# Retention and ELU feed-forward on one core: q decayed on GpSimd, outputs copied out of PSUM by ScalarE

## The chip, the core and the metric

The kernel runs on one core of a Trainium2 chip. The metric is the device time of one execution in microseconds (us). The engines are TensorE (PE in the profile, with its weight loads as PEld), VectorE (DVE), ScalarE (ACT), GpSimd (POOL) and SyncE (SP), which issues the DMAs.

## What is computed

The reference is a recurrent retention block followed by a feed-forward block with an ELU. Batch is 4, there are 8 heads of 64 channels, the sequence is 768 long; the 3072 tokens of 512 channels then pass through 512 x 2048 and 2048 x 512 weights.

```python
gamma = 1.0 - 2.0 ** (-5.0 - np.arange(H))
for t in range(S):
    state = gamma * state + k[:, :, t] (x) v[:, :, t]      # outer product, per head
    y[:, :, t] = scale * q[:, :, t] @ state
x = y.transpose(0, 2, 1, 3).reshape(B * S, H * D)
h = x @ w_in
g = np.where(h > 0.0, h, np.exp(np.minimum(h, 0.0)) - 1.0)
out = g @ w_out
```

## The kernel before

The tokens are worked off in six blocks of 512 (`tb` 0 to 5), each of four chunks of 128 tokens. A chunk's q, k and v lie in one tile `chunk` (128 x 2048 float32; four buffers), loaded by one DMA; q and k are in it with channels on the partitions, v and a second k with tokens on the partitions.

The decay is not applied step by step. With positions counted within a sequence, v is multiplied by gamma to the power of minus its position (`scale_v`, line 286, table `vf`), and the result of retention by gamma to the power of its position. The second factor lies in the table `etab` (128 x 4 x 768), which `powers_of` (line 254) fills with ScalarE exponentials at the start: first its first 256 columns, later the other 512. Retention of a block is `scores` (products of k and q, masked by VectorE), `states` (products of k and v added to a running state) and `outputs` (for each pair of chunks, products into two PSUM tiles `y`, first within the chunk, then against the states). At the end of `outputs`, line 398, VectorE multiplies each `y` with its piece of `etab` and writes the block's feed-forward input, `xb` (or `xt` for block 1).

Work is ordered by hand (a manual schedule): each engine runs its instructions in the order in which the program's generators are interleaved. Retention of block tb + 1 is placed in steps between the feed-forward products of block tb.

Block 0's first product is plain: `plain_first` makes 16 tiles of 128 x 512, each of four 128 x 512 matmuls (lines 511 and 535). The PSUM banks go round: tiles 0 to 3 use pa, pa, pb, pd (pa is two buffers), tile 4 a bank called hp, tiles 5 to 8 again pa, pa, pb, pd, and so on. Each tile is followed by `elu`: two ScalarE instructions (line 491 a Relu out of the bank into `r`, line 492 an Exp), and, one tile later in VectorE's order, line 495, which reads `r` and the bank and so releases it. Between the tiles the weights of the feed-forward block are decoded: `prepare` (lines 164 to 168, ScalarE) and `decode` (lines 190 to 194, VectorE) work on pieces `wraw`. GpSimd scales the four v chunks of block 1 there.

Later blocks use two levels of Strassen's scheme with products of 128 x 128 (lines 885 and 973) and of 128 x 256 (line 931); ScalarE copies `ms` and `m` and VectorE additions (lines 899, 939, 985) empty their banks, VectorE subtractions (lines 847, 944) make their inputs. In the loop over blocks `bring(n)` loads chunk n of the next block and has GpSimd scale its v.

Of the kernel before, what the change touches and what calls it, by code (L numbers as in the profile page):

```python
# [9 lines left out]
FP32 = mybir.dt.float32  # L10
# [3 lines left out]
AF = mybir.ActivationFunctionType  # L14
ALU = mybir.AluOpType
# [3 lines left out]
def kernel(  # L19
# [32 lines left out]
    nc = tc.nc  # L52
    PSUM = bass.MemoryType.PSUM
    P = nc.NUM_PARTITIONS

    B, H, S, D, DM, DFF = dims
    NTOK = B * S
    C = P
    TB = 512
    TH = TB // 2  # L60
    HP = H // 2
    NCH = S // C
    NCHUNK = NTOK // C
    NTB = NTOK // TB
    CPB = TB // C
# [3 lines left out]
    scale = 1.0 / math.sqrt(D)  # L69
# [143 lines left out]
    for a in range(2):  # L213
        for u in range(2):
            for c in range(2):
                nc.vector.memset(lny[c * D : (c + 1) * D, a, u : u + 1], math.log(gammas[head(a, u, c)]))
    pos_s = const.tile([P, NCH, H], I32, name="pos_s")
    nc.gpsimd.iota(pos_s, pattern=[[C, NCH], [0, H]], base=0, channel_multiplier=1)
    begin = so_.rearrange("p n s c -> p (n s c)")
# [26 lines left out]

    post = begin[:, S : 2 * S]
    nc.vector.tensor_copy(post, pos_t)
    etab = const.tile([P, 2, 2, S], FP32, name="etab")

    def powers_of(tokens):
        for a in range(2):
            for u in range(2):
                nc.scalar.activation(etab[:, a, u, tokens], post[:, tokens], AF.Exp, scale=lny[:, a, u : u + 1])

    powers_of(slice(0, 2 * C))

# [22 lines left out]
    def scale_v(m, by_vector=False):  # L280
        if m >= NCHUNK:
            return
        i = chunks[m][1]
        v = raw[m][1][:, 0]
        eng = nc.vector if by_vector or m < 2 else nc.gpsimd
        eng.tensor_tensor(  # L286
            out=v, in0=v, in1=vf[:, i].unsqueeze(2).to_broadcast([C, H, D]), op=ALU.mult
        )

    rows = lambda n: slice(n * D, (n + 1) * D)  # L290

# [86 lines left out]
    def outputs(tb, pp):  # L378

        y = [ps_r.tile([P, 2 * 2, 2, D], FP32, name="y", tag="r") for _ in range(2)]  # L380
        for x in range(2):
            for j in range(4):
                pt = raw[tb * CPB + 2 * pp + j // 2][0][:, 1].rearrange("p h c -> p (h c)")
                within(tb, pp, x, j, y, lambda p: pt[:, (x * HP + p) * D :][:, 0:D])
        for other in range(2):
            if not other:
                yield
            else:

                for sub in range(2):  # L390
                    seen = epool.tile([P, 8], FP32, name="seen", tag="seen")
                    nc.vector.tensor_copy(seen.rearrange("p (j x) -> p j x", x=2), y[sub][:, :, :, 0])
                yield
            for x in range(2):
                across(tb, pp, x, other, y)
        i = chunks[tb * CPB + 2 * pp][1]
        for sub in range(2):
            nc.vector.tensor_tensor(
                out=place_of(x_of(tb)[:, :, 2 * pp * C : 2 * (pp + 1) * C])[:, :, :, sub, :], in0=y[sub],
                in1=place_of(powers[:, :, i * C : (i + 2) * C])[:, :, :, sub, :], op=ALU.mult,  # L400
            )

    def within(tb, pp, x, j, y, pt):
        kv = raw[tb * CPB + 2 * pp + x][1]
# [759 lines left out]
    take()  # L1164
    state_sum(kvs, 0, 0, 1, 1)
    prepare(2)
    powers_of(slice(2 * C, S))
    next(inner)
    piece = decode()
    take()  # L1170
# [36 lines left out]
    for n, _ in enumerate(inner):  # L1207
        if n in (0, 2, 4):
            load(CPB + n // 2)
        if n == 4:  # L1210
            load(CPB + 3)
        if n in (1, 2, 4, 5, 7, 9):
            next_piece(n in (1, 2, 5, 7))
        if n in (3, 5, 7, 9):
            scale_v(CPB + (n - 3) // 2)
        if n == 4:
            run(inputs_of_first(0, [hslot() for _ in range(3)]))
        elif n == 10:
            scores(1, 0)
            scores(1, 1)  # L1220
        elif n == 11:
            states(1, 0)
            states(1, 1)
            next_piece()
            parts = sums_of_pieces(0)
            next(parts)
        elif n == 12:
            outputs_step(1, 0)
            run(parts)
            next_piece()  # L1230
        elif n == 13:
            outputs_step(1, 1)
            smalls = small_of_pieces(0)
            some(smalls, 3)
        elif n == 14:
            outputs_step(1, 2)
            some(smalls, 2)
            decode_all()
        elif n == 15:
            run(smalls)  # L1240
# [63 lines left out]
    for n in range(NQ):  # L1304
        if n < 3:
            load(2 * CPB + n)
        if n == 2:
            load(2 * CPB + 3)
        cur = first(n)
        for at in range(3):  # L1310
            next(cur)

        if n in (1, 2):
            some(smalls[n + 1], 1)
        elif n == 3:
            scale_v(2 * CPB, True)
        for _ in tail:
            pass
        for at, s in enumerate(cur):
            next(sides[n], None)  # L1320
            next(sides[n], None)
            if at == 1 and n in (0, 2):
                some(smalls[2 if n == 0 else 3], 2)
            elif at == 1 and n == 3:
                for m in range(1, CPB):
                    scale_v(2 * CPB + m, True)
            if s == "gap":
                break
        for _ in sides[n]:
            pass  # L1330
        tail = cur
        if n in (1, 2):
            run(smalls[n + 1])
        send_small()
# [28 lines left out]
    for tb in range(2, NTB):  # L1363
        more = tb + 1 < NTB
        qa, qd, u2, end = {}, {}, {}, None

        def rest(n, j):
            if j == 1:
                qa[n] = ps_r.tile([P, 2, TH], FP32, name="qa", tag="r") if n == 0 else bank("a")
            if j == 7:  # L1370
                qd[n] = ps_r.tile([P, 2, TH], FP32, name="qd", tag="r") if n == 3 else bank("bd"[n % 2])
            first_rest(n, j, qa[n] if j in (1, 6, 5) else qd[n])

        def bring(n):
            if more:
                load((tb + 1) * CPB + n)
                scale_v((tb + 1) * CPB + n)

        def pop(count=1):
            for _ in range(count):  # L1380
                if later:
                    later.pop(0)()

        bring(0)
        rest(0, 1)
        for _ in tail:
            pass
        tail, parts = iter(()), combine_x_parts()
        for at, j in enumerate(TWICE):
            cur = first_twice(tb, j)  # L1390

            next(cur)
            next(tail, None)
            next(parts, None)
            next(cur)
            for _ in tail:
                pass
            next(parts, None)
            if at == 1:

                first_end(0, "C11", qa[0])()
                bring(1)
            next(cur)
            tail = cur
        next(tail)
        bring(2)

        sec = second_twice(tb, combine_x_twice if more else lambda: None)
        for n in range(NQ):

            rest(n, 6)
            u2[n] = kept(qa[n])
            if n == 0:
                for _ in tail:
                    pass
            if end:
                end()
            pop()
            rest(n, 7)
            m7 = kept(qd[n])  # L1420
            pop(2)
            if n == 2 and more:
                retention_step(tb + 1, 1)
            if n == 3:
                next(sec)
            rest(n, 5)
            end = first_end(n, "C12", qa[n])
            other = first_end(n, "C22", qa[n], m7)
            if n < 3:
                end()  # L1430
                other()
                rest(n + 1, 1)
                first_end(n + 1, "C11", qa[n + 1])()
                rest(n, 4)
                end = first_end(n, "C21", qd[n], u2[n])
                pop()
                if n == 0:
                    bring(3)
                elif n == 1 and more:
                    retention_step(tb + 1, 0)  # L1440
        for _ in range(2):
            next(sec)
        end()
        other()
        rest(3, 4)
        end = first_end(3, "C21", qd[3], u2[3])
        next(sec)
        end()
        flush()
        step = 0  # L1450
        for s in sec:

            if s == "first":
                step += 1
            elif s != "middle" and step in (1, 4, 5):
                retention_step(tb + 1, {1: 2, 4: 3, 5: 4}[step])
            if s == ORDER2[-1]:
                break
        tail = sec
# [51 lines left out]
```

## Time and profile before

| what | value |
|---|---|
| three runs | 632.18, 632.34, 633.39 us; median 632.34 us |
| span of the profiled execution, first to last instruction | 631.6 us |
| the execution's own time beside the span | not given apart; the median lies 0.74 us above the span |
| TensorE busy | 623.8 us, 99% |
| VectorE busy | 482.1 us, 76% |
| ScalarE busy | 255.3 us, 40% |
| GpSimd busy | 22.1 us, 4% |
| granted TensorE clock | 0.999 |
| line 398, `y` times `etab` on VectorE | 22 instructions of 128 x 512, 0.68 us each |
| line 286, v scaling on GpSimd | 16 instructions of 128 x 512, mean 1212 ns |

Times in a row of a timeline are: start within the span, duration, engine, line, operation, output from input, shape, count, and in brackets the idle time before it with what ended it. A group of instructions that follow one another is one row. Busy shares of TensorE come from modelled ends of pipelined matmuls.

### The profile page before, as it was taken

What the parts mean: (1) busy time and instruction counts of PE and PEld (TensorE: products, weight loads), DVE (VectorE), ACT (ScalarE), POOL (GpSimd) and SP (SyncE); (2) the same over time, 40 slices, a digit from 0 to 9 for tenths busy, and PEclk for the clock granted to TensorE, in tenths of its full rate; (3) what the DMA queues carried; (4) which work ended last, traced back from release to release, by engine and by line L of the source; (5) the groups of instructions that cost most, each with busy time, mean ns of one, the idle gap of its engine ahead of it and who ended that gap; (6) DMA issues with size and microseconds to landing.
All of it is one profiled execution on the core that took longest, in us unless ns stands there. A gap on an engine that the chain in (4) does not pass through costs nothing.

```text
span 631.6 us, 16140 instructions
## 1 busy us (share of the span) xinstructions
PE 623.8 (99%) x6678; PEld 560.5 (89%) x6678; DVE 482.1 (76%) x882; ACT 255.3 (40%) x476; POOL 22.1 (4%) x30
## 2 busy tenths in 40 slices
PE   8999999999999999999999999999999999999997
PEld 6864578888899999888999989999989999988997
DVE  6688789989799665799585589777489877558975
ACT  6798646025541114553112646112465211366311
POOL 1021000000000000200000100000110000000000
PEclk9999999999999999999999999999999999999999
DMA  8698669699288788306888702889810698700794
GB/s 329 260 416 295 186 202 268 196 272 319 113 266 257 234 258 315 141 2 199 257 258 296 278 2 71 268 280 289 317 64 16 220 310 252 207 17 4 239 309 151
DMA packets 75897, 136.32 MB, mean 216 GB/s; under 512 B 6320, under 2 KB 31792, under 8 KB 70832
## 3 DMA queue, kind: packets, MB, share of 16 engines
q1 hardware_dynamic: 75824, 135.29, 64.9%
q8 instruction: 53, 0.87, 0.5%
q14 instruction: 20, 0.16, 0.1%
HBM read 114.03 MB, written 21.23 MB: 214 GB/s over the span
## 4 chain that ended last, share of the span: by engine, by line
PE 98%; DVE 0%; issue 0%; ACT 0%
PE pa L973 20%; PE pa L931 10%; PE pd L973 10%; PE pb L973 5%; PE pa L885 5%; PE pb L931 4%; PE pa L758 4%; PE pa L535 3%; PE qa L931 3%; PE x L625 3%; PE pd L885 2%; PE qd L931 2%; PE pd L931 2%; PE pd L758 2%; PE pa L625 2%; PE kv L352 2%
## 5 line engine op out<-in xcount | busy, mean ns | idle before, releaser
L981 ACT COPY ms<-pa 128x128 f32<-128x128 f32 x104 | 27.6, 265 | 148.2 <-PE pa L973 148.2
L973 PE MATMUL pa<-ts,wq 128*128 128x128 f32 x560 | 74.2, 275 | 0.0
L973 PE MATMUL pd<-ts,wq 128*128 128x128 f32 x552 | 73.5, 276 | 0.0
L973 PEld LDWEIGHTS pa<-ts,wq 128*128 128x128 f32 x560 | 68.5, 192 | 0.4
L973 PEld LDWEIGHTS pd<-ts,wq 128*128 128x128 f32 x552 | 67.1, 192 | 0.6 <-DVE res L985 0.2
L973 PE MATMUL pa<-gC,wq 128*128 128x128 f32 x480 | 64.6, 278 | 0.0
L492 ACT ACTIVATE r<-r 128x512 f32<-128x512 f32 x96 | 60.5, 631 | 3.1
L973 PEld LDWEIGHTS pa<-gC,wq 128*128 128x128 f32 x480 | 59.0, 192 | 1.3
L491 ACT ACTIVATE r<-gC 128x512 f32<-128x512 f32 x64 | 39.9, 624 | 31.9 <-DVE gC L939 31.9
L985 DVE TENSOR_TENSOR res<-pd,ms 128x128 f32<-128x128 f32 x68 | 19.5, 287 | 39.6 <-PE pd L973 38.4
L495 DVE SCALAR_TENSOR_TENSOR gC<-r,gC 128x512 f32<-128x512 f32 x64 | 42.6, 697 | 0.7 <-ACT r L492 0.7
L847 DVE TENSOR_TENSOR ts<-gC,ts 128x512 f32<-128x512 f32 x60 | 41.3, 688 | 1.0
L847 DVE TENSOR_TENSOR ts<-gC 128x512 f32<-128x512 f32 x60 | 41.0, 683 | 0.0
L286 POOL TENSOR_TENSOR chunk<-chunk,vf 128x512 f32<-128x512 f32 x16 | 19.4, 1212 | 429.6 <-DMA chunk<-in_qkv_dram 429.6
L973 PE MATMUL pb<-gC,wq 128*128 128x128 f32 x240 | 31.7, 275 | 0.0
L1006 ACT COPY res<-pa 128x128 f32<-128x128 f32 x34 | 9.0, 265 | 55.1 <-PE pa L973 55.1
L973 PEld LDWEIGHTS pb<-gC,wq 128*128 128x128 f32 x240 | 29.2, 192 | 0.0
L704 ACT COPY m<-pa 128x512 f32<-128x512 f32 x24 | 14.0, 582 | 33.0 <-PE pa L758 18.7
L939 DVE TENSOR_TENSOR gC<-qa,gC 128x512 f32<-128x512 f32 x8 | 5.5, 692 | 25.0 <-PE qa L931 18.3
L931 PE MATMUL pa<-xt,w_s 128*128 128x256 f32 x96 | 23.0, 382 | 0.0
L931 PE MATMUL pa<-xt,w_b 128*128 128x256 f32 x96 | 23.0, 382 | 0.0
L931 PE MATMUL pa<-xb,w_a 128*128 128x256 f32 x96 | 22.7, 379 | 0.0
(262 smaller groups left out, 1247.4 us busy)
## 6 DMA issues: line engine op xcount, KB each, us to landing
wq<-scratch_dram SPq DMA_DIRECT2D x277, 256.0 KB, 4.4
chunk<-in_qkv_dram SPq DMA_DIRECT2D x22, 1024.0 KB, 8.7
wraw<-in_w_dram SPq DMA_DIRECT2D x15, 1024.0 KB, 6.0
out_dram<-res SPq DMA_DIRECT2D x14, 256.0 KB, 4.1
scratch_dram<-gT SPq DMA_DIRECT2D x12, 256.0 KB, 4.3
scratch_dram<-m SPq DMA_DIRECT2D x12, 192.0 KB, 6.1
scratch_dram<-so SPq DMA_DIRECT2D x4, 512.0 KB, 4.7
scratch_dram<-wi SPq DMA_DIRECT2D x2, 1024.0 KB, 6.5
```

The costliest lines, as they stand in the source:

```text
L286: eng.tensor_tensor(out=v, in0=v, in1=vf[:, i].unsqueeze(2).to_broadcast([C, H, D]), op=ALU.mult)
L491: nc.scalar.activation(e, h, AF.Relu, scale=-1.0)
L492: nc.scalar.activation(e, e, AF.Exp, scale=-1.0)
L495: nc.vector.scalar_tensor_tensor(g, e, -1.0, h, ALU.add, ALU.max)
L625: nc.tensor.matmul(X[j][:, d, :], lhsT=w[j][:, d * P : d * P + P], rhs=x[j], start=(n == 0 and d == 0), stop=at_end, skip_group_check=True,)
L758: nc.tensor.matmul(ps[:, fi, :], lhsT=w[:, fi, j2, :], rhs=x[:, j2, :], start=(begin and fi == 0 and j2 == 0), stop=(j2 == 1), skip_group_ ...
L847: sub = lambda o, x, y: nc.vector.tensor_tensor(out=o, in0=x, in1=y, op=ALU.subtract)
L885: nc.tensor.matmul(ps[:, f, :], lhsT=lhs[f], rhs=xs[j][k], start=(begin and f == 0), stop=True, skip_group_check=True,)
L931: nc.tensor.matmul(ps[:, fi, :], lhsT=w[:, fi, j2, :], rhs=x[:, j2, :], start=(j in (1, 7) and fi == 0 and j2 == 0), stop=(j2 == 1), skip_ ...
L973: nc.tensor.matmul(ps, lhsT=w[:, f, :], rhs=ts[j][k][:, f, :], start=(begin and f == 0), stop=(f == 3), skip_group_check=True,)
L981: nc.scalar.copy(m, ps)
L985: nc.vector.tensor_tensor(out=o, in0=x, in1=y, op=ALU.add)
```

## The change

From block 1 on, the factor of q moves from the output to q itself. A new table `qtab` (128 x 4 x 768) holds gamma to the power of the position in q's layout; `scale_q` multiplies a chunk's q with it on GpSimd. In the loop over blocks it is called right behind `scale_v`. Block 1's four calls and the table's four exponentials stand between the tiles of block 0's plain product; block 2's four calls stand in the last quarter of block 1's first product. `outputs` then writes `y` with a plain ScalarE copy for every block but block 0. `etab` needs 512 columns only and is laid into a buffer that is used otherwise later.

```diff
+    lnq = const.tile([P, HP], FP32, name="lnq")
+    for a in range(2):
+        for p in range(HP):
+            nc.vector.memset(lnq[a * D : (a + 1) * D, p : p + 1], math.log(gammas[2 * p + a]))
...
-    etab = const.tile([P, 2, 2, S], FP32, name="etab")
+    etab = gq["T3"].rearrange("p (a u x) c -> p a u (x c)", a=2, u=2)
+    qtab = const.tile([P, HP, S], FP32, name="qtab")
...
+    def powers_for_q(p):
+        nc.scalar.activation(qtab[:, p, :], post, AF.Exp, scale=lnq[:, p : p + 1])
...
+    def scale_q(m):
+        if m >= NCHUNK:
+            return
+        i = chunks[m][1]
+        q = raw[m][0][:, 0]
+        nc.gpsimd.tensor_tensor(out=q, in0=q, in1=qtab[:, :, i * C : (i + 1) * C], op=ALU.mult)
...
+        tokens = slice(2 * pp * C, 2 * (pp + 1) * C)
         for sub in range(2):
-            nc.vector.tensor_tensor(
-                out=place_of(x_of(tb)[:, :, 2 * pp * C : 2 * (pp + 1) * C])[:, :, :, sub, :], in0=y[sub],
-                in1=place_of(powers[:, :, i * C : (i + 2) * C])[:, :, :, sub, :], op=ALU.mult,
-            )
+            to = place_of(x_of(tb)[:, :, tokens])[:, :, :, sub, :]
+            if tb:
+                nc.scalar.copy(to, y[sub])
+            else:
+                nc.vector.tensor_tensor(
+                    out=to, in0=y[sub], in1=place_of(powers[:, :, tokens])[:, :, :, sub, :], op=ALU.mult
+                )
...
-    powers_of(slice(2 * C, S))
+    powers_of(slice(2 * C, TB))
...
         if n in (3, 5, 7, 9):                       # between the tiles of the plain product
             scale_v(CPB + (n - 3) // 2)
+            scale_q(CPB + (n - 3) // 2)
+        if n in (0, 1):
+            powers_for_q(2 * n)
+            powers_for_q(2 * n + 1)
...
         elif n == 3:                                # block 1's first product
             scale_v(2 * CPB, True)
+            for m in range(CPB):
+                scale_q(2 * CPB + m)
...
                 scale_v((tb + 1) * CPB + n)         # bring(n) in the loop over blocks
+                scale_q((tb + 1) * CPB + n)
```

More of the change, by code (lines that the diff above doesn't have):

```diff
@@ L395, in outputs @@
                 across(tb, pp, x, other, y)
-        i = chunks[tb * CPB + 2 * pp][1]
+        tokens = slice(2 * pp * C, 2 * (pp + 1) * C)
         for sub in range(2):
-            nc.vector.tensor_tensor(
-                out=place_of(x_of(tb)[:, :, 2 * pp * C : 2 * (pp + 1) * C])[:, :, :, sub, :], in0=y[sub],
-                in1=place_of(powers[:, :, i * C : (i + 2) * C])[:, :, :, sub, :], op=ALU.mult,
-            )
+            to = place_of(x_of(tb)[:, :, tokens])[:, :, :, sub, :]
[5 more added lines that the diff above has]
+                )
     def within(tb, pp, x, j, y, pt):
```

## The prediction

> **What bounds the kernel now.** I read the page first (busy shares, chain), then the waits of TensorE, then the timelines of ScalarE and VectorE where those engines have no idle time, and last TensorE around the same moments.
>
> ```profile
> PE 623.8 (99%) x6678; PEld 560.5 (89%) x6678; DVE 482.1 (76%) x882; ACT 255.3 (40%) x476; POOL 22.1 (4%) x30
> ...
> PE 98%; DVE 0%; issue 0%; ACT 0%
> ```
>
> The chain that ended last is TensorE for 98% of the span. The change leaves TensorE's instructions and their order as they are, so it can act only through time in which TensorE waits. TensorE's list of waits:
>
> ```profile
> PE pa L1124 <- DVE blank L208: 1.5, 1, 1.5
> PE y L423 <- issue: 1.3, 1, 1.3
> PE pd L423 <- DVE seen L440: 0.5, 2, 0.3
> ```
>
> After start-up (first 30 us) only the 1.3 us row remains, a pause with no visible releaser at 298 us. So no VectorE relief, however large, has a wait to remove there: 22 output evictions of about 0.68 us hide under TensorE today. What has to be found is a place where the added or moved work makes TensorE wait. The page's slices (ScalarE 40% busy overall) do not show one; a window table does:
>
> ```profile
> 37.00:51.00 14.00, 14.00 (x35) 6.24 (x34) 11.39 (x15) 13.74 (x18) 5.92 (x4) 1.00 1.00 423
> ```
>
> Columns after the window: TensorE, weight loads, VectorE, ScalarE, GpSimd. Between 37 and 51 us ScalarE is busy 13.74 of 14 us. This is block 0's plain first product, and here the change puts four new ScalarE instructions, the q tables. ScalarE and VectorE there:
>
> ```profile
> 32.33 0.60 ACT L491 ACTIVATE r<-pa 128x512 f32<-128x512 f32 x1 [0.47 <-PE pa L511]
> ...
> 39.48 0.57 ACT L491 ACTIVATE r<-pd 128x512 f32<-128x512 f32 x1
> 40.09 0.63 ACT L492 ACTIVATE r<-r 128x512 f32<-128x512 f32 x1
> ```
> ```profile
> 40.75 0.69 DVE L495 SCALAR_TENSOR_TENSOR gC<-r,pd 128x512 f32<-128x512 f32 x1 [2.40 <-ACT r L492]
> 41.36 0.69 DVE L190 TENSOR_SCALAR wraw<-wraw 128x1024 f32<-128x1024 f32 x1
> 42.08 0.71 DVE L191 TENSOR_SCALAR wraw<-wraw 128x1024 uint32<-128x1024 uint32 x1
> 42.82 1.94 DVE L194 CUSTOM_DVE_ANT_0 w_b<-wraw,w_b 128x2048 uint16<-128x2048 uint16 x1
> ...
> 48.06 0.94 DVE L191 TENSOR_SCALAR wraw<-wraw 128x1024 uint32<-128x1024 uint32 x1
> 49.03 1.23 DVE L194 CUSTOM_DVE_ANT_0 w_a<-wraw,w_a 128x2048 uint16<-128x2048 uint16 x1
> 50.17 1.28 DVE L495 SCALAR_TENSOR_TENSOR gC<-r,pa 128x512 f32<-128x512 f32 x2
> ```
> ```profile
> 47.61 3.60 PE L535 MATMUL pd<-xb,w_a 128*128 128x512 f32 x8
> 51.04 3.60 PE L535 MATMUL pa<-xb,w_a 128*128 128x512 f32 x8
> ```
>
> VectorE waits 2.40 us for ScalarE's exponential of tile 3 (bank pd), and from 40.75 on has no idle time until both ELU ends at 50.17. The first of these two releases the bank pa that TensorE fills again from 51.04. It ends at 50.17 + 0.68 = 50.85: TensorE is 0.19 us from waiting. This is the thinnest slack I found after start-up.
>
> **The change, part by part.** *q tables.* Four exponentials of 128x768, two behind tile 0's ELU (before the row at 32.33), two before tile 2's. The trace has four of 128x256 in 1.70 us and four of 128x512 in 2.55 us: 0.21 us more each per 256 columns, so 0.64 + 0.21 = 0.85 us for 768, 3.40 us for four. The only gap ahead of tile 3 is the 0.47 us at 32.33, so tile 3's exponential comes 2.93 us late and VectorE's 40.75 becomes 43.68, since nothing else holds it. From there its order up to 50.17 is unchanged: 9.42 us, of which 0.95 us are not work: L194 at 42.82 took 1.94 instead of 1.23 and L191 at 48.06 took 0.94 instead of 0.70, both while a GpSimd scaling ran (42.15 for 1.54, 47.20 for 1.24). With p the price of one table instruction and c the GpSimd collisions of the new run, TensorE's wait is S = 4p - 0.47 - 0.95 + c - 0.19 = 4p + c - 1.61.
>
> *c.* Block 1's q scalings come behind the v scalings on GpSimd, so seven or eight GpSimd instructions fall between 37 and 54 us instead of four. Lower end 0; upper end three more at 0.71 each, 2.1. I take 0.5: the v scaling at 42.15 now falls into VectorE's longer idle time (its 0.71 goes) and its q scaling mostly too, while those from 47.2 to 52 meet VectorE instructions again, as the 0.24 one did. S = 3.40 + 0.5 - 1.61 = 2.3 us; ends 1.8 and 3.9.
>
> [...]
>
> TensorE stays serial behind this wait, and I found no later wait that would absorb it. Next late is tile 6's pa bank (VectorE 0.6 us behind, TensorE 3.4 us): covered.
>
> *Start-up.* Eight memsets of lnq go ahead of the position cast on VectorE. The lny row is 0.77 us for eight, the lng row 0.12; lnq has lny's shape but changes partition half once: I take 0.45. They delay the first four exponentials (4.25 to 5.95); the ScalarE copy on the start chain begins at 6.27, so 0.32 is free: +0.13 us, ends 0 and 0.45. The second set is halved (-0.85 us at 17.5), but ScalarE then waits 2.07 us for a DMA: nothing.
>
> *Outputs.* VectorE loses four evictions per block from block 1 on, 20 in all, x 0.68 = 13.6 us: worth nothing, as TensorE waits for none. ScalarE gains 20 copies at 0.58 (the 128x512 copy m<-pa, 582 ns). Queued behind four of them (2.33 us) stands one copy ms of the next inner product: in block 4 the y matmuls end near 528.3, the copies near 530.6, ms 0.27 later, and TensorE writes that bank again at 532.0. Cover 1.1 us; 0 taken. Block 1's copies run from about 80.5 to 83, TensorE's next bank is due at 84.3: 0.
>
> *q scaling in blocks 2 to 5.* 16 more GpSimd instructions at 1.04 (1.59 when disturbed). In block 3's loop the last v scaling starts at 361.64, so q is ready by 364.3 at worst; the scores start at 367.6. Block 2's four have loads issued up to 148.5 and at most 12 us in flight; even if they stood behind VectorE's v scalings (last at 176.4) they end by 181.3 or, disturbed, 183.5, against scores at 185.8. The SP queue's DMAs do not change. Collisions cost VectorE about 0.82 each (the 361.72 row of L944: 1.51 instead of 0.69), and VectorE then waits for TensorE 0.34 + 1.03 us a little later: covered. Without that cover, 12 x 0.82 = 9.8 us is the outer end; I give it no weight beyond 0.3 us in the upper rival.
>
> **Sum.** 631.6 (span) + 2.3 + 0.13 = 634.0. The median of the runs, 632.34, lies 0.74 above the span, so 634.8.
>
> **Rivals.** *Nothing reaches TensorE.* If a 768-column exponential cost no more than 0.40 us, S = 0 without collisions; that is the point from which this decides. For it: long instructions have a fixed part. Against: the 512 row is already 0.64. It gives 631.6 + 0.13 + 0.74 = 632.5, no change. The same verdict comes if the 1.25 us pause at 298 us (no releaser) is absent after: 633.5, within the threshold. Getting clearly faster would need both; nothing in the waits pays for it.
>
> *Upper.* Collisions decide: c = 2.1, start-up 0.45, 0.3 in the later loops: 631.6 + 3.9 + 0.45 + 0.3 + 0.74 = 637.0. For it: VectorE is saturated exactly where GpSimd's work doubles. Against: before, only two of four scalings cost it anything.
>
> *VectorE relief pays.* The page's 76% VectorE and a ScalarE at 40% speak for moving evictions, but only if a TensorE wait ended on VectorE; the waits list has none after start-up. It would give at most 632.34 - 1.3 = 631.0.
>
> **How the numbers follow.** Stall of 1.8 to 3 us: 0.64. Nothing reaches TensorE or the pause goes: 0.16. Upper: 0.15. Faster: 0.05. About 0.2% (1.26 us) is what a measurement of this kernel can tell from no change; 634.8 is 2.5 us above, so slower 0.64 + 0.15 = 0.79. The range goes from the no-stall case, less 0.3, to the upper rival plus 0.4.
>
> **What would show it.** Right: TensorE's waits gain one row, pa of the first product waiting for VectorE's ELU end, 1.8 to 3.9 us, near 51 us; four 128x768 ScalarE rows near 0.85 us at 32 to 39 us; VectorE's wait for tile 3's exponential grows from 2.4 to about 5 us; from there everything runs later by a constant. Wrong: no such row; or a wait of the scores for GpSimd, or of an inner product for a ScalarE copy, at each block; or VectorE ending its stretch to 50.17 on time.

## The result and the profile after

The changed kernel takes 641.62 us (median of four runs, 638.47 to 642.24) against 632.3 us, which is 9.3 us or 1.5% between the medians. The ratio that goes with the interval, which is not the quotient of the medians, is 1.0122 (1.0094 to 1.0151). The kernel is slower, as predicted, but by 9.3 us instead of 2.5, and all four runs lie above the predicted range (632.2 to 637.4).

In every run here the time is the span plus about 1.8 us (1.73 to 1.90). The profiled execution of the changed kernel has a span of 640.4 us and a time of 642.13 us. The page of before (span 631.6 us) therefore belongs to its run of 633.39 us, not to its median; a span for the median would be about 630.5 us. The two pages differ by 8.8 us.

From the page of after: busy shares of the engines, the TensorE clock in 40 slices (tenths of full speed), and the chain that ended last.

```profile
PE 627.2 (98%) x6678; PEld 562.1 (88%) x6678; DVE 482.7 (75%) x870; ACT 267.4 (42%) x500; POOL 49.3 (8%) x50
...
PEclk9997999999999999999999999999999999999999
...
PE 94%; DVE 2%; ACT 2%; issue 1%; DVEq 0%
```

The chain ran over TensorE for 98% of the span before. Now 2% each of VectorE and ScalarE have come into it, so somewhere TensorE waits for them. The fourth slice (48 to 64 us) shows a clock of 0.7. TensorE's waits, longest first (total, times, longest, us):

```profile
PE pa L554 <- DVE gC L514: 5.0, 1, 5.0
PE pa L1143 <- DVE blank L208: 1.5, 1, 1.5
PE pd L777 <- DVE h L728: 0.8, 1, 0.8
PE y L427 <- issue: 0.8, 1, 0.8
PE y L442 <- issue: 0.6, 1, 0.6
```

The second row was there before. The first is the predicted one, at the predicted place: bank pa of the plain first product, tile 9, waiting for VectorE's ELU end. It took 5.03 us instead of 2.3. The third is new; the prediction had put block 2's scalings at nothing. Tile 9 itself (the trace has two records for each matmul, so x8 is one tile of four):

```profile
57.53 6.05 PE L554 MATMUL pa<-xb,w_a 128*128 128x512 f32 x8 [5.03 <-DVE gC L514]
```

The same eight records took 3.60 us before, so 2.45 us more are lost behind the wait. The windows around it (columns after the window: TensorE, weight loads, VectorE, ScalarE, GpSimd, then the granted clock, DMA share, GB/s):

```profile
55.00:58.00 3.00, 0.47 (x1) 0.47 (x2) 2.97 (x5) 2.38 (x4) 0.07 (x1) 0.58 0.19 30
58.00:60.00 2.00, 2.00 (x3) 0.70 (x3) 1.93 (x4) 1.97 (x3) 0.00 (x0) 0.50 0.80 279
60.00:62.00 2.00, 2.00 (x4) 0.72 (x3) 2.00 (x4) 0.08 (x1) 0.00 (x0) 0.50 0.65 229
62.00:64.00 2.00, 2.00 (x6) 1.02 (x5) 1.93 (x3) 0.39 (x1) 0.00 (x0) 0.93 0.78 311
```

The clock falls to 0.50 while TensorE waits, and stays there for the next 4.8 us of matmuls. At half clock these lose half of that, 2.4 us, which is the 2.45.

The difference of 8.8 us between the two profiled runs is found in five places. The start-up is 1.29 us longer, as the second halves of tiles 0 and 1 show, first before, then after:

```profile
28.68 3.62 PE L511 MATMUL pa<-xb,w_a 128*128 128x256 f32 x16
```
```profile
29.97 3.62 PE L530 MATMUL pa<-xb,w_a 128*128 128x256 f32 x16
```

The wait adds 5.03, the slow tile 2.45, and the wait in block 1 0.8. The pause at 298 us, 1.25 before, is 0.6 now. 1.29 + 5.03 + 2.45 + 0.8 - 0.65 = 8.9.

How the wait grew is seen on three engines. ScalarE, the tables (two in a row) and the exponential of tile 3:

```profile
33.06 1.75 ACT L262 ACTIVATE qtab<-so,lnq 128x768 f32<-128x768 f32 x2
...
38.28 1.74 ACT L262 ACTIVATE qtab<-so,lnq 128x768 f32<-128x768 f32 x2
...
44.06 0.63 ACT L511 ACTIVATE r<-r 128x512 f32<-128x512 f32 x1
```

GpSimd, scalings of v (L294) and q (L304) of block 1:

```profile
43.93 1.04 POOL L294 TENSOR_TENSOR chunk<-chunk,vf 128x512 f32<-128x512 f32 x1 [2.36 <-DMA chunk<-in_qkv_dram]
44.93 1.27 POOL L304 TENSOR_TENSOR chunk<-chunk,qtab 128x512 f32<-128x512 f32 x1
48.98 1.27 POOL L294 TENSOR_TENSOR chunk<-chunk,vf 128x512 f32<-128x512 f32 x1 [2.78 <-DVE w_b L194]
50.21 1.72 POOL L304 TENSOR_TENSOR chunk<-chunk,qtab 128x512 f32<-128x512 f32 x1
51.90 1.49 POOL L294 TENSOR_TENSOR chunk<-chunk,vf 128x512 f32<-128x512 f32 x1
53.35 1.72 POOL L304 TENSOR_TENSOR chunk<-chunk,qtab 128x512 f32<-128x512 f32 x1
```

VectorE, from the ELU end of tile 3 to the one that releases bank pa:

```profile
44.72 0.69 DVE L514 SCALAR_TENSOR_TENSOR gC<-r,pd 128x512 f32<-128x512 f32 x1 [2.84 <-ACT r L511]
45.32 1.43 DVE L190 TENSOR_SCALAR wraw<-wraw 128x1024 f32<-128x1024 f32 x1
46.79 0.70 DVE L191 TENSOR_SCALAR wraw<-wraw 128x1024 uint32<-128x1024 uint32 x1
47.52 1.22 DVE L194 CUSTOM_DVE_ANT_0 w_b<-wraw,w_b 128x2048 uint16<-128x2048 uint16 x1
48.66 0.68 DVE L573 TENSOR_TENSOR h<-gC,gC 128x512 f32<-128x512 f32 x1
49.38 1.41 DVE L573 TENSOR_TENSOR gC<-gC 128x512 f32<-128x512 f32 x1
50.83 1.65 DVE L573 TENSOR_TENSOR h<-gC,gC 128x512 f32<-128x512 f32 x1
52.52 1.42 DVE L573 TENSOR_TENSOR h<-gC,h 128x512 f32<-128x512 f32 x1
53.86 0.68 DVE L514 SCALAR_TENSOR_TENSOR gC<-r,hp 128x512 f32<-128x512 f32 x1
54.45 1.16 DVE L191 TENSOR_SCALAR wraw<-wraw 128x1024 uint32<-128x1024 uint32 x1
...
56.79 1.28 DVE L514 SCALAR_TENSOR_TENSOR gC<-r,pa 128x512 f32<-128x512 f32 x2
```

Tile 3's exponential starts at 44.06, before at 40.09: 3.97 us later, of which 1.29 are the start-up and 2.68 the tables. The stretch on VectorE from 44.72 to 56.79 takes 12.07 us; the same work took 9.42 before, 0.95 of it collisions, so 8.47 undisturbed. That makes c = 3.6 us of collisions (time by which a VectorE instruction is longer while a GpSimd instruction runs): L190 at 45.32 lost 0.73, the three disturbed L573 0.72, 0.97 and 0.74, L191 at 54.45 0.46. Each of these rows overlaps a GpSimd row, and all five read their inputs from SBUF alone. The ELU end at 53.86, which reads one input out of a PSUM bank, overlaps one too and took 0.68, as it did before beside the scaling at 47.20 (row at 47.46). Together 2.68 + 3.6 - 0.95 - 0.19 = 5.1, against 5.03 measured.

### The profile page after: what moved, and what is told of

Its sections match the earlier page's. It is cut to its first block, busy times and chain, and to the rows that moved or that the text cites. A ratio compares the mean times of both kernels' runs of the same rounds, so it can differ in the third digit from the quotient of the medians.

```text
span 640.4 us, 16190 instructions
## 1 busy us (share of the span) xinstructions
PE 627.2 (98%) x6678; PEld 562.1 (88%) x6678; DVE 482.7 (75%) x870; ACT 267.4 (42%) x500; POOL 49.3 (8%) x50
## 4 chain that ended last, share of the span: by engine, by line
PE 94%; DVE 2%; ACT 2%; issue 1%; DVEq 0%
PE pa L992 20%; PE pa L950 10%; PE pd L992 10%; PE pb L992 5%; PE pa L904 5%; PE pa L777 4%; PE pb L950 4%; PE qa L950 3%; PE x L644 3%; PE pa L554 3%; PE pd L904 2%; PE pd L777 2%; PE qd L950 2%; PE pd L950 2%; PE pa L644 2%; PE kv L368 2%
## 5 line engine op out<-in xcount | busy, mean ns | idle before, releaser
L514 DVE SCALAR_TENSOR_TENSOR gC<-r,gC 128x512 f32<-128x512 f32 x64 | 45.4, 741 | 0.7 <-ACT r L511 0.7
L294 POOL TENSOR_TENSOR chunk<-chunk,vf 128x512 f32<-128x512 f32 x16 | 17.9, 1122 | 301.0 <-DMA chunk<-in_qkv_dram 287.4
L304 POOL TENSOR_TENSOR chunk<-chunk,qtab 128x512 f32<-128x512 f32 x20 | 28.8, 1442 | 112.4 <-DMA chunk<-in_qkv_dram 100.6
```

Of the source, the lines that this page charges most:

```text
L304: nc.gpsimd.tensor_tensor(out=q, in0=q, in1=qtab[:, :, i * C : (i + 1) * C], op=ALU.mult)
L514: nc.vector.scalar_tensor_tensor(g, e, -1.0, h, ALU.add, ALU.max)
```

## The experiments

Theory A (after the result): the exponentials make VectorE late by 2.7 us; GpSimd's scalings make it late by 2 to 4 us more; the TensorE wait that comes of both is followed by the halved clock (0.50); block 2's q scaling adds a smaller wait. Rival B: the tables alone make the loss, and the scalings add nothing. Rival C: part of the loss comes from the output copies or the later blocks. Rival D: relieving VectorE pays something. Rival E: the tile is slow because of what runs beside it, not because TensorE was idle. Edits are against the changed kernel unless said otherwise. A ratio is to the kernel before, run on the same chip beside it (632.3 us in one group, 632.9 us in the other; 632.74 us, a single run, beside the two repeats below and the nine memsets).

**The changed kernel twice more.**

> The changed kernel once more, for its spread (its four runs lie between 638.5 and 642.2 us). Theory: the wait at pa is 2.7 us of ScalarE's lateness plus the collisions c of this run minus 1.14 us; c depends on when the four chunk loads land against VectorE's instructions, so it differs (3.6 us in the profiled run, 2.5 and 1.5 in two experiments): a wait between 3 and 5.2 us, with the clock drop behind it if the run is at 640 us or more. Rival: always 5.0 us, and the spread comes from elsewhere.

> A second look at the changed kernel for its spread. Theory: wait at pa = 2.7 + c - 1.14 us with c read from VectorE's lengthened instructions of this run, between 3 and 5.2 us. Rival: always 5.0 us.

One run each, 638.43 and 640.23 us. Tile 9 in the first and in the second:

```profile
55.05 5.40 PE L554 MATMUL pa<-xb,w_a 128*128 128x512 f32 x8 [3.56 <-DVE gC L514]
```
```profile
56.36 6.04 PE L554 MATMUL pa<-xb,w_a 128*128 128x512 f32 x8 [4.80 <-DVE gC L514]
```

The added durations of VectorE's rows in the stretch give c = 2.1 and 3.4. With 2.68 + c - 1.14 the waits should be 3.6 and 4.9; they are 3.56 and 4.80. Between these two the spread is that of c and of the clock behind it: the wait differs by 1.24 us and tile 9 by 0.64, together 1.9 us, and the runs by 1.8. The profiled run of 642.13 us is longer than the second by its start-up and a pause, 0.9 and 0.6 us, more than by its wait. Which VectorE instructions the GpSimd scalings meet goes with when they start; of the eight in the first profile two waited for a chunk's DMA (those at 38.20 and 43.93), one for the table (40.10) and one for VectorE (48.98). The clock falls to 0.50 in both.

**The tables moved into ScalarE's gaps.** Two of the exponentials go behind the second fill of `etab`, two behind the `prepare` ahead of the tile loop.

```diff
     powers_of(slice(2 * C, TB))
+    powers_for_q(0)
+    powers_for_q(1)
...
     prepare()
+    powers_for_q(2)
+    powers_for_q(3)
...
-        if n in (0, 1):
-            powers_for_q(2 * n)
-            powers_for_q(2 * n + 1)
```

> The four q-table exponentials go into ScalarE's two idle stretches before tile 0 (the DMA wait near 20 us and the wait for tile 0's matmuls near 30 us, 2 us each in the changed kernel's trace); GpSimd's q scalings stay. Theory A (ScalarE's lateness and GpSimd's collisions add): ScalarE is on time, VectorE is still stopped by the scalings for about 3.6 us as in the changed kernel, less 1.14 us of slack: TensorE waits 2.5 us at the first product's pa, 632.3 + 2.5 + 0.8 (a wait in block 1's first product) = 635.6 us, up to 1 us more if the granted clock falls. Rival B (ScalarE's tables alone make the wait): no wait there, 633.1 us.

635.89 us, ratio 1.0056 (1.0034 to 1.0078). Tile 9:

```profile
52.88 3.70 PE L554 MATMUL pa<-xb,w_a 128*128 128x512 f32 x8 [1.27 <-DVE gC L514]
```

Here c was 2.5, and 2.5 - 1.14 = 1.4 against a wait of 1.27 without any table in the way. Rival B would have had no wait. The granted clock is 1.00 in every window from 52 to 60 us, and the tile has nearly its old length. The wait is half of what I expected, because c was lower than in the first profile. One of the other three runs, 637.26 us, was granted only 0.997 of the clock; no trace of it was kept.

**The tables left, block 1's q scalings removed** (block 1's q then lacks its decay).

```diff
-            scale_q(CPB + (n - 3) // 2)
```

> The tables stay where the change has them, block 1's four q scalings are left out (block 1's q then lacks its decay). Theory A: ScalarE 3.3 us of tables, only the v scalings collide (0.95 us): 3.30 + 0.95 - 1.61 = 2.6 us of wait, 632.3 + 2.6 + 0.8 = 635.7 us, up to 1 us more for the clock. Rival B: the whole 5.0 us wait and the slow matmuls after it stay, 641 us.

637.43 us, ratio 1.0091 (1.0058 to 1.0124). The wait is 1.84 us with c = 0.43: 2.66 late + 0.43 - 1.14 = 1.95.

```profile
54.04 3.70 PE L554 MATMUL pa<-xb,w_a 128*128 128x512 f32 x8 [1.84 <-DVE gC L514]
```

The clock stays at 1.00 again. So in the profiles each half alone leaves a wait of 1.3 to 1.8 us at full clock; together they make 3.6 to 5 us and a halved clock. That is not so in every run. Two of this kernel's five, 638.41 and 642.47 us, were granted 0.997 and 0.995 of the clock, and so was, at 0.997, the one run with the tables in the gaps. All six runs of the changed kernel were at 0.994 to 0.997, and no run of the kernel before was under 0.999. So the clock can fall with one half alone as well, if less often, and it does so now and then with neither (one run each of the next two kernels). The time of the profiled run is not explained by its wait alone: its TensorE list also has 0.9 us in block 1 and two pauses without a releaser, 1.5 and 0.7 us.

**Both.**

> Both at once: tables in ScalarE's idle stretches, block 1's q scalings left out (block 1's q lacks its decay). What is left of the change is ScalarE's output copies, block 2's q scaling and the later ones, the memsets. Theory A: no wait at the first product's pa; 632.3 plus the 0.8 us wait in block 1's first product, 633.1 us. Rival C (the later blocks' copies and scalings cost too): 635 us or more.

633.54 us, ratio 1.0023 (1.0007 to 1.004). No wait on pa is left in the profile. What is left is the wait in block 1's first product:

```profile
PE pd L777 <- DVE h L728: 1.4, 1, 1.4
```

**Both, and block 2's q scalings removed too** (blocks 1 and 2 then lack q's decay).

```diff
-            for m in range(CPB):
-                scale_q(2 * CPB + m)
```

> As the third experiment (tables in ScalarE's idle stretches, no q scaling of block 1), and block 2's four q scalings are left out too (blocks 1 and 2 lack q's decay). What stays: 20 output copies on ScalarE, VectorE relieved of them, q scalings of blocks 3 to 5. Theory A (the rest of the change is free and VectorE's relief is worth nothing): the 1.4 us wait at pd in block 1's first product is gone, 632.3 us, ratio 0.999 to 1.001. Rival C (later scalings or copies cost): 633.5 us or more. Rival D (VectorE's relief pays): 631.5 us or less.

633.13 us against 632.9, ratio 1.0000 (0.9985 to 1.0016). The row on pd is gone. The 20 output copies on ScalarE, the q scalings of blocks 3 to 5 and the 20 instructions fewer on VectorE are all still in this kernel, and together they cost or bring no more than 0.16%, 1 us. Rivals C and D fall to within that. One run of these twelve (636.68 us) and one of the ten before (638.0 us) were still granted 0.997; what lowered it in them is open, as no trace of them was kept.

The ladder of ratios is then: 0% with no early q scaling and the tables in gaps, 0.23% with block 2's, 0.56% with block 1's as well, 1.22% with the tables in the way too. Only the last step is clear of the intervals; the first three overlap in turn, and what tells them apart is the wait that comes or goes in the profile. By ratios the parts simply add up: block 2's 0.23, block 1's scalings alone 0.33 and the tables alone 0.68 make 1.24.

**TensorE kept busy in the wait.** Ahead of tile 9 five matmuls, whose result nobody reads, go into a bank that is free there; they take 4.3 us of TensorE themselves.

```diff
+            if k == 4:
+                idle = ps_r.tile([P, 2, TH], FP32, name="idle", tag="r").rearrange("p a b -> p (a b)")
+                unread(5, TB, idle)
```

> The changed kernel with five unread 128x512 matmuls (4.3 us) ahead of tile 9, inside TensorE's 5.0 us wait. If the slow matmuls after the wait (6.05 us instead of 3.60 for tile 9, granted clock 0.50 from 58 to 62 us) come from TensorE having stood idle: tile 9 takes 3.6 us again, 641.6 - 2.4 = 639.2 us. If something else slows them: 641.6 us, unchanged.

639.45 us, ratio 1.0118 (1.0091 to 1.0144). TensorE in the plain product:

```profile
51.79 4.46 PE L1146 MATMUL idle<-blank 128*128 128x512 f32 x10
56.08 3.60 PE L557 MATMUL pa<-xb,w_a 128*128 128x512 f32 x8
```

Without the filler TensorE would have waited 3.0 us here (from 51.79 until VectorE's release at 54.10 + 0.68). With it tile 9 is back at 3.60 us, and VectorE and GpSimd still work and collide beside it (L194 at 52.01 took 2.18 us, L190 at 55.30 took 1.58): rival E falls. The other three runs, 638.84 to 639.49 us, were granted the full clock and lie at the 639.2 expected. The ratio does not show a gain, since the added matmuls take longer than the wait, and since the profiled run (642.48 us) has a second loss, in block 1's first product:

```profile
169.76 2.77 PE L780 MATMUL pd<-xb,w_s 128*128 128x256 f32 x8 [1.95 <-DVE h L731]
172.33 2.84 PE L780 MATMUL pa<-xb,w_b 128*128 128x256 f32 x8
```

These eight take 1.89 us in the tiles around them. Here a wait of 1.95 us, on the bank that block 2's scalings delay, was followed by half clock (0.50 from 170.84 to 174.25), which shows in these two rows.

**A wait of chosen length in the kernel before.** Six, nine and twelve VectorE memsets stand in the same stretch, with nothing of the change in the kernel. Each took 0.48 us, but they start 0.66 us apart, so the waits of six and twelve came out longer than expected.

```diff
+            if k == 1:
+                for _ in range(6):                  # 9, 12 in the others
+                    nc.vector.memset(gq["T3"][:, 0:2, :], 0.0)
             elu(g_plain[row * NF + 2 * n + fi], hp)
```

> The kernel before with six VectorE memsets of 128x512 (0.48 us each, 2.9 us) ahead of the ELU end that releases bank pa for tile 9. Theory (a wait of TensorE costs its length, and beyond some length more, because the granted clock falls to half for some us): a wait of about 2.6 us; the changed kernel had no drop behind waits of 1.3 and 1.8 us, a drop behind 2.0 and 5.0, so here a drop is likely: tile 9 takes 4.5 to 6.1 us instead of 3.6. Rival (the clock fell for another reason): 3.6 us.

> The kernel before with nine VectorE memsets ahead of the same ELU end; six gave a wait of 3.5 us and tile 9 in 6.5 us, twelve 7.5 and 5.6. Theory (the clock falls about 3 us into a wait and stays at half for some 6 us, so a longer wait covers more of it): a wait of 5.4 us, tile 9 in 6.0 us, span near that of twelve less 1.7. Rival (a short wait is cheaper per us): tile 9 in 4 us.

> The same with twelve memsets (5.8 us): a wait of about 5.5 us without any of the change's instructions. Theory: granted clock 0.50 after it, tile 9 in 5.5 to 6.5 us as in the changed kernel, span 8 us above the kernel before (5.5 + 2.4). Rival: tile 9 in 3.6 us, span 5.5 us above.

One run each: 638.51, 639.97 and 641.51 us, with waits of 3.51, 5.47 and 7.55 us at tile 9. With six, nine and twelve memsets:

```profile
54.44 6.51 PE L535 MATMUL pa<-xb,w_a 128*128 128x512 f32 x8 [3.51 <-DVE gC L495]
```
```profile
57.39 5.51 PE L535 MATMUL pa<-xb,w_a 128*128 128x512 f32 x8 [5.47 <-DVE gC L495]
```
```profile
58.85 5.61 PE L535 MATMUL pa<-xb,w_a 128*128 128x512 f32 x8 [7.55 <-DVE gC L495]
```

Against 3.60 us, tile 9 is 1.9 to 2.9 us longer, so each wait costs that much more than its length. The times, against 632.9 and 632.74 us beside them, are 5.6, 7.2 and 8.6 us longer, 1.1 to 2.1 us more than the wait; single runs of the kernel before differ by up to 2.8 us, so the tile is the better measure. In all three the clock was at 0.50 for 6.8 us: the drop comes with the wait and needs none of the change's instructions.

**The whole change, in another order.** Tables in the gaps; block 1's four q scalings behind all its v scalings; block 2's moved to its next v scalings and held back there by a one-element copy on GpSimd that reads `gq["C11"]`.

```diff
+        if n == 9:
+            for m in range(CPB):
+                scale_q(CPB + m)
...
+                nc.gpsimd.tensor_copy(sink, gq["C11"][0:1, 6, 0:1])
+                for m in range(CPB):
+                    scale_q(2 * CPB + m)
```

> The whole change, complete, with only the order mended: tables in ScalarE's idle stretches; block 1's four q scalings behind its four v scalings on GpSimd; block 2's four held back on GpSimd until the ELU of block 1's last quarter (C11) is there. Theory A (the loss is collisions on VectorE where TensorE waits for it, plus ScalarE's lateness): VectorE is in time for pa, no wait at pd: 632.3 to 632.9 us. Rival C (20 more GpSimd multiplications cost wherever they are): 634 us or more.

633.81 us against 632.9, ratio 1.0008 (0.9999 to 1.0018). There is no wait on pa; one of 1.1 us remains later (bank pd of block 1's second product). GpSimd's four q scalings now run in one piece, and VectorE beside them:

```profile
51.15 6.86 POOL L305 TENSOR_TENSOR chunk<-chunk,qtab 128x512 f32<-128x512 f32 x4
```
```profile
51.39 1.58 DVE L190 TENSOR_SCALAR wraw<-wraw 128x1024 f32<-128x1024 f32 x1
53.01 1.65 DVE L191 TENSOR_SCALAR wraw<-wraw 128x1024 uint32<-128x1024 uint32 x1
54.69 2.18 DVE L194 CUSTOM_DVE_ANT_0 w_b<-wraw,w_b 128x2048 uint16<-128x2048 uint16 x1
```

VectorE loses about as much in these three rows as in the changed kernel's stretch (0.88 + 0.95 + 0.95 = 2.8 us, there 2.1 to 3.6), but behind the ELU end that TensorE waits for, where it has slack. With every added instruction still there the loss goes from 1.2% to 0.1%. It does not beat the kernel before.

## Why the prediction was right or wrong

**Place and direction: right.** The change acted through one thin slack on VectorE in block 0's plain product, at bank pa; no VectorE relief was to be had elsewhere.

**The tables (4p - 0.47 = 2.93): right, within 0.25 us.** One exponential of 768 columns costs 0.825 us (33.06 to 34.71 for two) against the 0.85 taken, and tile 3 came 2.68 us late. The rival "nothing reaches TensorE" needed 0.40 us or less.

**c: the term that was mis-sized.** I took 0.5 with an upper end of 2.1; the three profiles of the changed kernel have 3.6, 2.1 and 3.4. The failing sentence is that most of the q scaling behind 42.15 would fall into VectorE's idle time, "while those from 47.2 to 52 meet VectorE instructions again, as the 0.24 one did". The first v scaling did fall into idle time (43.93 to 44.97), but its q scaling met L190 and cost 0.73, and the two later pairs cost 0.46 to 0.97 where I took 0.24 as their measure. That 0.24 was the smaller of the two collisions in that stretch before; the other, 0.71, is close to the mean of the five measured, 0.72, and the prediction itself priced a collision in a later block at 0.82. Even the upper end was no bound: it priced three more collisions at 0.71, but the sum had already taken the old 0.95 out, so three more would have made 3.1, and a wait of 3.40 + 3.1 - 1.61 = 4.9. That is near the measured 3.6 and 5.03 of the first profile, with five collisions in place of the old two, and near the 3.4 and 4.80 of the third (2.1 and 3.56 in the second).

**The clock: a term that the sum lacked.** It adds 2.45 us to tile 9 in the first profile, 1.80 and 2.44 in the two others. With c = 3.1 but without this term the prediction would have been 637.4, still below every run.

**Block 2's scaling at 0: wrong.** I only asked whether q is ready for the scores, and not what GpSimd does to VectorE while TensorE runs close behind. In the first profile two rows of VectorE, in a stretch without idle time, met it:

```profile
162.25 1.80 DVE L707 TENSOR_TENSOR w_s<-w_a,w_s 128x512 f32<-128x512 f32 x1
...
168.42 1.60 DVE L514 SCALAR_TENSOR_TENSOR gC<-r,h 128x512 f32<-128x512 f32 x1
```

They take 0.69 and 0.68 undisturbed. The wait on pd was 0.5 to 2.0 us in the profiles with these scalings in their old place. Without them its row is gone; the ratios, 1.0023 and 1.0000, have intervals that overlap.

**The price of a q scaling: too low.** I took the v scaling's 1.04 us; the shortest of the changed kernel's 20 take 1.27. Whether VectorE loses more beside the longer instruction was not tried by itself.

**Start-up: +0.13 predicted; the memsets cost nothing.** They take 0.21 us and the ScalarE copy behind them begins at 6.29 against 6.27. The profiled run does lose 1.29 us there. The two others, at 28.97 and 29.03, lie within what the kernels without the change show (28.39 to 29.39). In the first, 0.8 is a pause without a releaser, which neither of the others has and whose cause is open; 0.41 I put down to the clock at the start (last section).

**The base: 0.74 us between span and median.** This was a wrong pairing, since the profiled execution was before's slowest run and its time, 633.39, lies 1.8 above its span. It did no harm to the forecast: 631.6 + 0.74 is the median, and 2.3 + 0.13 added to the median is the same 634.8.

**The copies, blocks 3 to 5, VectorE's relief: right at 0**, to within 0.16%, by the kernel without early q scalings.

**Rivals.** The upper one named the right mechanism (collisions decide) but was priced at 637.0; with the clock and block 2 its own wait of 3.9 would have made about 640. "VectorE relief pays" fell. "Nothing reaches TensorE" fell with the first row of the waits.

## What to carry to other kernels

Work on GpSimd was not free beside a saturated VectorE here (0.46 to 0.97 us for each row of VectorE that it lengthened in the first stretch): count each GpSimd instruction at the typical collision seen in the trace, not at the smallest, and place it where VectorE has slack behind the last thing that TensorE waits for. When a sum says that TensorE will wait about 2 us or more, add what the clock then takes: here the profiled waits of 1.95 us and more were all followed by half clock, which took 1.8 to 2.9 us on the tiles behind them. Before trusting slack, look at how thin it is at every place where added work lands, not only at the place where its result is needed.

## What was not expected of the hardware

- **The clock drop had two lengths.** By the traces' record of the granted clock, and by half-microsecond windows, the clock was at 0.50 for 6.8 us in the first profile of the changed kernel (55.46 to 62.29), in its third and in all three with memsets, and for 3.4 us in its second (55.78 to 59.19) and in block 1 of the kernel with filler matmuls (170.84 to 174.25). In the five with 6.8 us TensorE stood idle for 1.1 to 3.2 us more behind the fall of the clock; in the two with 3.4 us it had been at work again for 0.73 and 1.08 us when the clock fell. No run tries what sets the length.
- **A wait of 1.95 us was followed by the drop, one of 1.84 us was not.** When the clock fell, TensorE had been idle for 1.95 us in the filler kernel and for 2.3 to 4.6 us in the six others, and the wait had begun 2.3 to 4.6 us earlier. The waits of 1.27 us (tables in the gaps) and 1.84 us (tables left) passed at a clock of 1.00, and so did the 1.5 us pause of the latter kernel. What decides between 1.84 and 1.95 us is not shown; no run tries it, and both are single waits.
- **Collisions cost both sides.** GpSimd's q scalings beside the lengthened L573 rows took 1.72 us, where the shortest take 1.27; the longest, 2.27 us at 51.09 in the kernel with the tables in the gaps, stands beside an L194 of 1.96 us instead of 1.23.
- **Pauses of TensorE without a releaser** (0.2 to 1.5 us, at `y`, `kv`, hp and pa) come and go between runs of the same kernel. No run here tells what they are.
- **The start-up matmuls met the clock at different places before and after.** I put 0.41 us of the first profile's start-up down to that. The scores' matmuls before and after:

```profile
6.16 0.69 PE L312 MATMUL sc<-chunk 64*64 64x64 f32 x32
```
```profile
6.19 1.13 PE L328 MATMUL sc<-chunk 64*64 64x64 f32 x32
```

In the clock record the first full-clock stretch begins at 6.08 us before and at 7.68 after. The record has no value ahead of that stretch, so a lower clock there is an estimate from the lengths of these rows (0.69 and 1.13 us). Whether it goes with the change is not shown.
